# A fixed table of operations in place of a list scheduler, and ReLU and square in one tile

## Chip, core, metric

One core of a Trainium2 chip. The metric is the device time of the kernel in microseconds (us), as the median of several runs.

## What is computed

Linear attention with cosine weights, followed by a feed-forward layer with a squared ReLU. Everything arrives in float32; the kernel multiplies in bfloat16.

```python
q, k, v: (8, 8, 576, 64)           # batch, heads, positions, head size
w_in: (512, 2048)   w_out: (2048, 512)

theta = pi / 2 * pos / S
phi(x) = concat([relu(x) * cos(theta), relu(x) * sin(theta)], -1)
kv  = einsum('bhsf,bhsd->bhfd', phi(k), v)
z   = sum over s of phi(k)
num = einsum('bhsf,bhfd->bhsd', phi(q), kv)
den = einsum('bhsf,bhf->bhs', phi(q), z) + 1e-6
x = (num / den), as 4608 tokens of 512
out = (relu(x @ w_in) ** 2) @ w_out
```

## The kernel before

**Work and names.** The kernel handles the eight batches one after another, each 512 tokens ("main"); the last 64 positions of all batches ("tails") are gathered as a ninth block, number 8. Every piece of work is an operation of a planner (`plan.op`) with a name, the engines that may run it and a cost on each, the operations that it follows, and the buffers that it holds. The engines are TensorE (PE), VectorE (DVE), ScalarE (ACT), GpSimd (POOL) and SyncE (SP). Names for batch b:

- `ldk`, `ldq`, `ldv`, `ldkt`, `ldqt`: loads of k, q, v and of the tails of k and q, issued by SP (by POOL for the first batches). k and q share one buffer (`kq`), of which there is one, so a batch's load waits for the last feature of the batch before.
- `vs`: v spread into the operand of the attention product; `cosb.j`, `sinb.j` (`fe` in the profile, lines 525 and 527): the features of k and q for a quarter of the positions, on ACT or DVE; `.t` is the tail.
- `qTd`, `xTd`: transposes by DMA on SP's queue; `qT`, `xT` with `qTc`, `xTc`: transposes by TensorE and the copy behind them (the first two batches).
- `kv`, `kvz`: the sum of phi(k) v, and its copy; `num`, `div`: the numerator on TensorE and the division on DVE (three instructions).
- `Hb.s.th`: a plain product x @ w_in for tokens half t and half h of the hidden units, block s (batches 0, 1 and half of 2), with its ReLU `r` and its square `q`.
- `Gb.s`: the same for four such products by a seven-product scheme (Strassen's form, as Winograd rearranged it): `P1` to `P7` on TensorE, `seed`, `u2`, `s5` copies out of PSUM between them, and four results `c11`, `c12`, `c21`, `c22`, each with a ReLU `r` and a square `q`. `xs` are the sums of blocks of x, `w1s`, `w2t` those of the weights.
- `Yb`: the second product, by the same scheme: `S1` to `S4` are sums of blocks of the squares, `P1` to `P7` the products, `seed`, `u2`, `s5`, `c..` the copies, `st0`, `st1` the stores. In batch 0 it is plain: `Y0.0` to `Y0.15`. Batch 8's last products, copies and stores are cut in halves.

A product of a G block is four 128x256 matmuls, one of a Y block sixteen. `yb`, `ya`, `hb`, `ha`, `hc`, `hps` in the profile are the PSUM tiles of these products. There are six PSUM banks of the kind that they use (pool `x`) and one more, two banks wide, for `kz` and `num` (pool `n`).

**ReLU and square.** `activate` (line 962) takes a tile `rt` from a pool of four, writes the ReLU of a product's 512 columns into it, and squares it into a part of `gT`, the operand of the second product: `gT` is laid out as token quarter, hidden block, 128 tokens, and the square turns the order:

```python
r = plan.op(f"{name}r", engines, lambda e: emit(e, rt[:, :, :]), after, bufs + [rt])
split = lambda ap: ap.rearrange("p h (t c) -> p t h c", t=2)
g_ready[b, tok, half, s] = plan.op(
    f"{name}q", both(act(2 * W), 0.34),
    lambda e: square(e, g[:, :, 2 * s : 2 * s + 2, :], split(rt[:, :, :])), [r], [rt, g])
```

There are 144 such squares. `gT` has eight blocks; a batch takes four.

**The order.** `Plan.timeline` gives each TensorE step a due time along a planned sequence, `Plan.dues` passes due times back to what it needs, and `Plan.run` (line 208) plays a list scheduler: at every moment each free engine takes, of the operations that are ready and whose buffers have room, the one with the earliest due time plus a hand-set shift (`SHIFT`); an operation that ACT and DVE can both do goes to the one that ends it first, or where `PINS` puts it. Each engine then runs its operations in that order, each waiting for what it needs, so that whatever stands behind a waiting instruction on the same engine waits too. The orders that come out, where they are spoken of below:

```
TensorE  H1.3.01 H1.1.00 num2.2 H1.3.11 H1.2.11 num2.3 Y1.P1 num2.0 Y1.P2 num1.4 Y1.P6 Y1.P5
TensorE  num3.2 G2.3.P1 G2.3.P5 Y1.P3 num3.3 G2.2.P7 G2.2.P3 xT1.4 Y1.P4 num2.4
         G2.3.P2 G2.3.P6 G2.2.P4 G2.3.P7 Y2.P1
TensorE  Y2.P7 G3.1.P4 G3.2.P2 num3.4 G3.2.P6 G3.3.P1 Y2.P3
DVE      G3.1.c22r sin5.0 G3.1.c22q G3.1.c21r Y2.c22
SP       qTd4.0 qTd4.1 xTd2.2 Y1.st1 ldqt6.0 ldv5.0 ldkt6.1 ldk5 ldq5 ldkt6.0
```

Of the kernel before, what the change touches and what calls it, by code (L numbers as in the profile page):

```python
# [17 lines left out]
FP = 512  # L18

LAG = {"PE": 0.21, "ACT": 0.15, "DVE": 0.14, "POOL": 0.15, "SP": 0.1}  # L20
SAME = 0.12
CARE = 1.0
ROOM = 2500
SHIFT = {
    "H0.0.00.0": 23.3, "H0.0.10.0": 65.1, "H0.2.10.0": 67.9, "H0.3.01.0": 100.8, "sin1.0": 16.7,
    "sin1.2": 46.1, "num1.0": 22.3, "qT1.3": -67.9, "num1.3": 71.9, "num1.4": 80.8,
    "Y0.13": 67.3, "ldv2.2": -46.8, "ldkt2.0": -47.2, "num2.0": 98.2, "xTd2.1": 24.1,
    "H1.0.10.0": 14.7, "H1.1.00.0": 64.8, "H1.2.00.0": -21.4, "H1.2.11.0": 97.2,
    "H1.3.01.0": 43.2, "H1.3.11.0": 93.2, "vs3.1": 33, "cos3.2": 20.4, "sin3.t": 42.9,
    "div3.4": 15.5, "xs2.2": 40.2, "H2.0.10.0": 15.6, "H2.0.01.0": -24.5, "H2.1.00.0": -45.7,  # L30
    "H2.1.01.0": 9, "H2.1.11.0": 5.4, "G2.2.u2": 38.7, "G2.2.P3": 32.8, "G2.2.c12q": 8.6,
    "G2.2.P7": 25.3, "G2.2.c22r": 2.7, "G2.3.seed": -10.2, "Y1.S4": 32.8, "Y1.P7": 7,
    "Y1.P3": 13.8, "Y1.c12": -77.9, "Y1.P4": 24, "vs4.1": 37.5, "sin4.0": -4.1, "cos4.1": 5.5,
    "sin4.2": -74.7, "sin4.3": -4.2, "num4.2": -19, "div4.4": 37.7, "xTd4.2": 147.6,
    "G3.0.P1": -10.2, "G3.0.P5": -64.2, "G3.0.P2": -4, "G3.0.P6": -9.8, "G3.0.P3": -41.8,
    "G3.0.P4": -12.3, "G3.1.P1": -64.3, "G3.1.seed": -8.5, "G3.1.P6": -36.7, "G3.1.P3": -20.1,
    "G3.2.P1": -23.4, "G3.2.P6": 12.1, "G3.2.c22r": 9.4, "G3.3.c11q": 22.3, "G3.3.c12r": 6.4,
    "G3.3.c22q": 19.6, "G3.3.c21q": 3, "Y2.P6": 3.7, "Y2.P5": -7.6, "Y2.P3": 15.5,
    "Y2.st0": 52.3, "Y2.st1": 80.4, "ldk5": 45.3, "ldq5": 53.1, "ldv5.0": 29.5, "vs5.1": 8.5,
    "cos5.0": 3.1, "div5.0": 17.6, "num5.1": 18.6, "div5.1": 47.3, "num5.4": 16, "G4.0.P5": 23.7,  # L40
    "G4.0.P3": -47.4, "G4.2.P1": 20.1, "G4.2.P2": 11.4, "G4.2.s5": 39.5, "G4.2.c12r": 1.7,
    "G4.2.P4": -80, "G4.3.P1": -53.6, "G4.3.P4": -11, "Y3.P6": 12.5, "Y3.P3": 16.9,
    "Y3.st0": 43.4, "Y3.st1": 134.8, "ldv6.0": 71.2, "ldv6.2": 38.3, "ldkt6.0": 32.6,
    "ldqt6.0": -5.7, "ldqt6.1": 37.9, "cos6.0": 38.4, "cos6.2": 46.4, "sin6.2": 28.5,
    "sin6.3": 32.6, "qTd6.1": 47.7, "num6.4": -23.5, "xs5.1": 11.7, "xs5.2": 3.2, "xs5.4": -19.2,
    "G5.0.P3": -36.7, "G5.1.P5": -13, "G5.1.c12r": 29.6, "G5.1.c22r": -21.5, "G5.2.P1": 3.5,
    "G5.2.P5": 8.1, "G5.2.P2": 1.8, "Y4.S4": -92.6, "Y4.S3": -85.2, "Y4.P1": -1.2, "Y4.P7": 35.4,
    "Y4.P5": -3.4, "ldk7": 116.4, "ldkt7.0": 40.2, "ldkt7.1": 34.3, "G6.0.P3": 49.7,
    "G6.1.P5": 41.4, "G6.2.P2": 47.4, "G6.2.P6": 48.2, "G6.2.P3": 68.3, "G6.2.c21r": 40.2,
    "G6.3.P5": 44.3, "G6.3.P2": 60.8, "Y5.P4": 42.1, "G7.0.P7": 38.8, "G7.1.P5": 46.8,  # L50
    "G7.2.P6": -13.6, "G7.3.P6": -4.6, "G7.3.c21r": 7, "Y6.P6": 65.2, "Y6.P7": 79.3,
    "Y6.P4": 26.7, "G8.0.P2": 34.1, "G8.0.s5": 3.7, "G8.1.P7": 33.7, "Y7.P6": 130.6,
    "Y7.P7": 241.7, "Y7.P4": 300.4,
}
EARLY = 20
STRETCH = 1.08
EARLY_TAIL = 15
REPORT = []
PLAIN = ((1, 0), (1, 1), (2, 0))
PINS = {  # L60
    "ACT": (
        "qTc0.3 H0.3.01q sin1.0 cos1.1 sin1.1 cos1.3 sin1.3 vs2.1 H1.0.11r H1.1.00r H1.3.01q "
        "sin3.0 cos3.3 cos3.t H2.0.01q H2.1.00r G2.3.u2 G2.3.s5 sin4.1 cos4.2 cos4.3 G3.0.s5 "
        "G3.1.c11q G3.2.c11r G3.3.c12q G3.3.c21r cos5.t sin5.t G4.0.c12q G4.1.c21q G4.2.u2 "
        "G4.2.c12q G4.3.c12q G4.3.c22q Y3.c21 vs6.1 sin6.1 cos6.3 G5.2.u2 G7.0.c12q Y7.s5"
    ),
    "DVE": (
        "vs3.1 cos3.2 G3.1.c21r G3.2.u2 cos5.1 cos5.2 cos5.3 G4.1.c11q G4.1.c22q G4.1.c21r "
        "G4.2.s5 G4.3.c21q cos6.0 cos6.2 G5.1.c22q G5.1.c21r G7.2.c22q G7.3.c21r Y6.u2 "
        "G8.0.c21r"  # L70
    ),
}
PIN = {n: e for e, names in PINS.items() for n in names.split()}
BIAS = 0
EITHER = ("ACT", "DVE")


class Buf:
# [3 lines left out]
    def __init__(self, pool, shape, dtype, name, kind=None):  # L82
        self.pool, self.shape, self.dtype, self.name, self.kind = pool, shape, dtype, name, kind
        self.users, self.left, self.slot, self.tile = [], 0, None, None
# [39 lines left out]
class Op:  # L124
    def __init__(self, name, engines, emit, after, bufs, due, done, slack, fixed):
        self.name, self.engines, self.emit, self.bufs = name, engines, emit, bufs
        self.after = [a for a in after if a is not None]
        self.due, self.done, self.slack, self.fixed = due, done, slack, fixed
        self.next, self.start, self.end, self.engine, self.late = [], None, None, None, None
        for a in self.after:  # L130
            a.next.append(self)
        for b in bufs:
            b.users.append(self)


class Plan:
# [3 lines left out]
    def __init__(self):  # L140
        self.ops, self.pools, self.fifo = [], {}, {}

    def pool(self, name, n, order=None):
        self.pools[name] = n
        if order is not None:
            self.fifo[name] = order

    def op(self, name, engines, emit, after=(), bufs=(), due=None, done=None, slack=0.0):
        o = Op(name, engines, emit, after, list(bufs), due, done, slack, None)
        self.ops.append(o)  # L150
        return o

    def given(self, name, at, bufs=()):

        o = Op(name, {}, None, (), list(bufs), 0.0, None, 0.0, at)
        self.ops.append(o)
        return o

    def timeline(self, chains, at):

        for row in chains:
            todo = [list(c) for c in row]
            size = max(len(c) for c in todo)
            taken = [0] * len(todo)
            for n in range(1, size + 1):
                for i, c in enumerate(todo):
                    while taken[i] < len(c) * n // size:
                        o, drains = c[taken[i]]
                        taken[i] += 1
                        o.due = at  # L170
                        at += o.engines["PE"] * STRETCH
                        for d, slack in drains:
                            d.due = at + slack

    def dues(self):

        after = {o: list(o.after) for o in self.ops}
        for p in self.fifo:
            made = self.order(p) if self.fifo[p] == 1 else []
            for old, new in zip(made, made[self.pools[p] :]):  # L180
                users = set(new.users)
                for o in new.users:
                    if not users.intersection(o.after):
                        after[o] += old.users
        later = {o: [] for o in self.ops}
        for o in self.ops:
            for a in after[o]:
                later[a].append(o)
        count = {o: len(later[o]) for o in self.ops}
        todo = [o for o in self.ops if not count[o]]  # L190
        while todo:
            o = todo.pop()
            if o.fixed is not None:
                continue
            took = min(o.engines.values())
            if o.done is not None:
                took += o.done[0] + CARE
            late = min((n.due - 0.15 for n in later[o]), default=1e6) - took
            if o.late is not None:
                late = min(late, max(a.due for a in o.after) + o.late)  # L200
            o.due = late if o.due is None else min(late, o.due)
            o.due -= o.slack
            for a in after[o]:
                count[a] -= 1
                if not count[a]:
                    todo.append(a)

    def run(self, free, dma=0.0):


        taken = {(b.pool, b.slot) for o in self.ops for b in o.bufs if b.slot is not None}
        slots = {
            p: [(0.0, i) for i in range(n) if (p, i) not in taken] for p, n in self.pools.items()
        }
# [4 lines left out]
        for o in self.ops:  # L219
            o.key = o.due + SHIFT.get(o.name, 0.0)  # L220
# [1426 lines left out]
```

## Time and profile before

| what | value |
|---|---|
| time, median of 3 runs | 277.29 us (277.2 to 278.34) |
| span of the profiled execution | 275.1 us |
| first matmul, of the warm-up | 1.2 us |
| last matmul starts | 270.8 us |
| idle time of ACT ahead of features, for q (the longest) | 6.7 us (3.3) |
| idle time of DVE ahead of features, for k and for q | 5.2 and 3.2 us |
| moved by DMA | 53.00 MB |

The span runs from the first to the last instruction of one execution; the time of a run has some two microseconds more around it. A row of the timeline or of the groups names the engine, the source line, the operation and the tiles it writes and reads; a bracket gives the idle time of the engine ahead of it and what ended that. Matmuls overlap, so their recorded time is longer than the distance between their starts. Many operations have one helper's line (538 is every matmul, 509 every copy), so they are told apart by their tiles and their order.

### The profile page before, as it was taken

What the parts mean: (1) busy time and instruction counts of PE and PEld (TensorE: products, weight loads), DVE (VectorE), ACT (ScalarE), POOL (GpSimd) and SP (SyncE); (2) the same over time, 40 slices, a digit from 0 to 9 for tenths busy, and PEclk for the clock granted to TensorE, in tenths of its full rate; (3) what the DMA queues carried; (4) which work ended last, traced back from release to release, by engine and by line L of the source; (5) the groups of instructions that cost most, each with busy time, mean ns of one, the idle gap of its engine ahead of it and who ended that gap; (6) DMA issues with size and microseconds to landing.
All of it is one profiled execution on the core that took longest, in us unless ns stands there. A gap on an engine that the chain in (4) does not pass through costs nothing.

```text
span 275.1 us, 6864 instructions
## 1 busy us (share of the span) xinstructions
PE 266.3 (97%) x2792; PEld 225.1 (82%) x2792; DVE 229.6 (83%) x449; ACT 190.3 (69%) x322; POOL 28.7 (10%) x47
## 2 busy tenths in 40 slices
PE   8999999999999999989999999999999999999994
PEld 2579746699798888968998999888988888888883
DVE  2778677998999899979999899989779889977931
ACT  5587791798698589779898877888358744665400
POOL 8834364100000000000000000000000000000000
PEclk9999999999999999999999999999999999999999
DMA  7999999999999997999986999483321001100125
GB/s 225 293 206 259 311 284 273 355 285 271 303 232 345 268 186 219 349 163 191 327 255 172 246 235 305 99 219 119 79 100 63 4 12 67 79 0 2 76 57 174
DMA packets 79198, 53.00 MB, mean 193 GB/s; under 512 B 52256, under 2 KB 74784, under 8 KB 79168
## 3 DMA queue, kind: packets, MB, share of 16 engines
q1 hardware_dynamic: 71488, 38.28, 54.5%
q0 software_dynamic: 7040, 13.76, 19.2%
q10 hardware_dynamic: 640, 0.52, 0.7%
q8 instruction: 22, 0.36, 0.5%
q14 instruction: 8, 0.07, 0.1%
HBM read 36.70 MB, written 9.44 MB: 168 GB/s over the span
## 4 chain that ended last, share of the span: by engine, by line
PE 69%; DMA 18%; DVE 4%; POOL 4%; ACT 3%; issue 1%; SPq 1%; DVEq 0%; POOLq 0%; ACTq 0%
PE ya L538 15%; PE yb L538 13%; PE hb L538 10%; DMA kq<-in_q_dram 7%; PE hc L538 7%; PE ha L538 7%; PE hps L538 6%; DMA w1sb<-in_moe_w_in_dram 5%; PE yh L538 4%; DMA kqt<-in_k_dram 3%; PE kz L538 2%; PE num L538 2%; DMA qpTt<-fet 2%; DVE gs L535 1%; PE yc L538 1%; ACT fe L525 1%
## 5 line engine op out<-in xcount | busy, mean ns | idle before, releaser
L538 PEld LDWEIGHTS <-w1sb 128*128 128x128 bf16 x736 | 70.1, 98 | 10.5 <-issue 2.4
L538 PEld LDWEIGHTS <-gs 128*128 128x128 bf16 x512 | 49.7, 98 | 6.1 <-DVE gs L535 0.4
L538 PEld LDWEIGHTS <-gT 128*128 128x128 bf16 x448 | 43.3, 98 | 10.7 <-issue 0.5
L519 ACT ACTIVATE gT<-rt 128x512 bf16<-128x512 bf16 x65 | 40.4, 630 | 8.5 <-DVE rt L532 7.0
L525 ACT ACTIVATE fe<-kq,cols 128x1024 bf16<-128x1024 f32 (+1 forms) x34 | 34.2, 1043 | 9.2 <-DMA kq<-in_q_dram 6.7
L538 PE MATMUL hps<-xT,w1sb 128*128 128x256 bf16 x320 | 37.5, 273 | 0.0
L521 DVE TENSOR_TENSOR gT<-rt 128x512 bf16<-128x512 bf16 x79 | 31.7, 420 | 3.5 <-ACT rt L513 3.1
L527 DVE TENSOR_SCALAR fe<-kq,cols 128x1024 bf16<-128x1024 f32 (+1 forms) x38 | 25.9, 718 | 8.4 <-DMA kq<-in_k_dram 5.2
L538 PEld LDWEIGHTS <-w1s 128*128 128x128 bf16 x312 | 29.8, 98 | 3.6
L538 PE MATMUL ya<-w2sb,gT 128*128 128x256 bf16 x256 | 30.7, 273 | 0.4 <-ACT yb L509 0.4
L538 PE MATMUL hb<-xs,w1sb 128*128 128x256 bf16 x208 | 30.4, 273 | 0.4 <-ACT u L509 0.2
L538 PE MATMUL ha<-xT,w1sb 128*128 128x256 bf16 x176 | 25.9, 273 | 1.3 <-DVE rt L515 1.2
L670 DVE TENSOR_TENSOR xp<-num,den 128x512 bf16<-128x512 f32 (+1 forms) x33 | 22.2, 675 | 1.1
L513 ACT ACTIVATE rt<-hps 128x512 bf16<-128x512 f32 x34 | 19.7, 596 | 4.5 <-PE hps L538 4.3
L535 DVE TENSOR_TENSOR gs<-gT 128x2048 bf16<-128x2048 bf16 x16 | 19.5, 1220 | 0.3 <-ACT gT L519 0.2
L532 DVE CUSTOM_DVE_ANT_0 rt<-hc,u 128x512 bf16<-128x512 f32 x26 | 17.6, 684 | 2.6 <-PE hc L538 2.6
L532 DVE CUSTOM_DVE_ANT_0 rt<-hb,s 128x512 bf16<-128x512 f32 x26 | 17.8, 686 | 1.4 <-PE hb L538 1.1
L513 ACT ACTIVATE rt<-ha 128x512 bf16<-128x512 f32 x23 | 13.7, 595 | 6.3 <-PE ha L538 6.3
L509 ACT COPY u<-hb 128x512 f32<-128x512 f32 x22 | 12.8, 583 | 4.9 <-PE hb L538 4.7
L509 ACT COPY s<-hc 128x512 f32<-128x512 f32 x20 | 11.8, 588 | 6.4 <-PE hc L538 6.3
L509 ACT COPY hb<-ha 128x512 f32<-128x512 f32 x26 | 15.3, 590 | 0.6 <-PE ha L538 0.3
L538 PE MATMUL hc<-xs,w1s 128*128 128x256 bf16 x104 | 15.6, 273 | 0.0
(112 smaller groups left out, 411.1 us busy)
## 6 DMA issues: line engine op xcount, KB each, us to landing
out_dram<-y SPq DMA_DIRECT2D x16, 512.0 KB, 4.3
vs<-in_v_dram SPq DMA_DIRECT2D x10, 512.0 KB, 4.9
kq<-in_k_dram SPq DMA_DIRECT2D x5, 1024.0 KB, 6.8
kq<-in_q_dram SPq DMA_DIRECT2D x5, 1024.0 KB, 9.0
w1sb<-in_moe_w_in_dram POOLq DMA_DIRECT2D x4, 512.0 KB, 11.5
w2sb<-in_moe_w_out_dram POOLq DMA_DIRECT2D x4, 512.0 KB, 11.2
kq<-in_q_dram POOLq DMA_DIRECT2D x2, 1024.0 KB, 10.9
kq<-in_k_dram POOLq DMA_DIRECT2D x2, 1024.0 KB, 11.4
```

Source lines behind the costliest of these rows:

```text
L509: (nc.scalar.copy if e == "ACT" else nc.vector.tensor_copy)(out=out, in_=in_)
L513: nc.scalar.activation(out=out, in_=in_, func=ACTF.Relu)
L519: nc.scalar.activation(out=out, in_=in_, func=ACTF.Square)
L521: nc.vector.tensor_tensor(out=out, in0=in_, in1=in_, op=ALU.mult)
L525: nc.scalar.activation(out=out, in_=in_, func=ACTF.Relu, scale=col)
L527: nc.vector.tensor_scalar(out=out, in0=in_, scalar1=0.0, scalar2=col, op0=ALU.max, op1=ALU.mult)
L532: nc.vector._custom_dve(dve_ops.TENSOR_ADD_SAT, out=out, in0=in0, in1=in1, s0=BIG, s1=0.0)
L535: nc.vector.tensor_tensor(out=out, in0=in0, in1=in1, op=op)
L538: nc.tensor.matmul(out=out, lhsT=lhsT, rhs=rhs, start=start, stop=stop, skip_group_check=True)
L670: nc.vector.tensor_tensor(out=x, in0=n4[:, :, :, 0:D].rearrange("p b (k l) d -> p b k l d", l=2), in1=r.rearrange("p b (k l) -> p b k l", l=2)
```

## The change

**The order is a table.** `SHIFT`, `PINS`, the due times, `timeline`, `dues`, `order` and the list scheduler go. A string `ORDER` lists all 1066 operations; a star puts one on ACT where ACT and DVE could both do it. `Plan.run` walks through it and only chooses the slot of each new buffer:

```diff
+    def run(self, table, free, dma=0.0):
+        ops = {o.name: o for o in self.ops}
+        order = []
+        for word in table.split():
+            o = ops.pop(word.rstrip("*"))
+            o.engine = "ACT" if word[-1] == "*" else min(o.engines, key=lambda e: e == "ACT")
+            order.append(o)
...
+        for o in order:
+            e = o.engine
+            t = max([free[e]] + [a.end + lag(a, e) for a in o.after])
+            for b in sorted((b for b in o.bufs if b.slot is None), key=lambda b: b.index):
+                t, b.slot = slot(b, t)
```

The estimated costs that the planner uses are set anew (`act(n)` from 0.14 to 0.08 us plus 0.00082 per element, `dve(n)` from 0.10 to 0.07 plus 0.00104, and the like); they now serve the choice of slots alone. Which products are plain and which are by the scheme stays as it was, and so does all that is issued ahead of the plan (`begin`, `loads_of_1`).

**ReLU and square in one tile.** `gT` is laid out as hidden block, token quarter, 128 tokens; the ReLU writes straight into it, and one square works in place on two neighbouring blocks. The pool `rt` goes.

```diff
-                gT[b, tok, half] = buf("g", [P, 2, HB2, P], BF16, "gT")
+                gT[b, tok, half] = buf("g", [P, HB2, 2, P], BF16, "gT")
...
-        rt = buf("rt", [P, 2, W], BF16, "rt")
         g = gT[b, tok, half]
-        r = plan.op(f"{name}r", engines, lambda e: emit(e, rt[:, :, :]), after, bufs + [rt])
...
+        many = SQUARES.get(b, 2)
+        r = plan.op(
+            f"{name}r", engines, lambda e: emit(e, g[:, 2 * s : 2 * s + 2, :, :]), after, bufs + [g]
+        )
+        group = squares.setdefault((b, tok, half, s // many), [])
+        group.append(r)
+        if len(group) < many:
+            return r
+        s0 = s // many * many
+        part = slice(2 * s0, 2 * (s0 + many))
...
+            lambda e: square(e, g[:, part, :, :], g[:, part, :, :]),
+            group,
+            [g],
```

`SQUARES` is empty, so `many` is 2 everywhere: 72 squares of 1024 elements a partition. The sums `gs` of the second product and its matmuls take the new layout; the matmuls are the same in number and size. The tile of zeros for the warm-up moves from the place of `rt` to that of `gs`.

**The order in the table**, at the places quoted above and at some others (the table isn't sorted by time; what counts is the order on each engine):

```
TensorE  H1.3.11 num2.2 H1.1.00 H1.2.11 num2.3 H1.3.01 Y1.P1 num2.0 Y1.P2 num1.4 Y1.P6 Y1.P5
TensorE  num3.2 Y1.P3 G2.2.P3 xT1.4 G2.2.P7 num3.3 G2.3.P1 Y1.P4 num2.4
         G2.3.P2 G2.3.P6 G2.3.P5 G2.2.P4 G2.3.P7 Y2.P1
TensorE  Y2.P7 G3.1.P4 num3.4 G3.2.P6 G3.2.P2 G3.3.P1 Y2.P3
TensorE  G4.3.P1 G4.2.P3 G4.3.P5 G4.3.P6      Y3.P7 G4.2.P6 G4.2.P2 num4.4 Y3.P4
TensorE  G7.3.P6 G7.2.P4 G8.0.P1 G7.3.P7
DVE      G3.1.c22r div4.3 sin5.1 G3.1.c21r cos5.2
ACT      sin4.0 G2.3.c11r G2.3.u2 G2.3.s5 Y1.c21 G2.2.c21r cos4.3 cos4.t G3.0.seed
ACT      G6.1.s5 G6.1.c11q G6.2.seed G6.1.c12q G6.3.seed    G6.3.c11q G7.0.seed    G7.3.c22q G8.0.seed
SP       qTd4.0 Y1.st0 xTd2.2 qTd4.1 ldv5.0 ldk5 ldq5 ldkt6.0 Y1.st1 xTd4.0
```

## Prediction

> **What bounds the kernel now.** I read the page's busy times first, then the table by stretches, then the TensorE timeline with its waits, then the queues behind the waits that are left.
>
> ```profile
> span 275.1 us, 6864 instructions
> PE 266.3 (97%) x2792; PEld 225.1 (82%) x2792; DVE 229.6 (83%) x449; ACT 190.3 (69%) x322; POOL 28.7 (10%) x47
> ```
>
> ```profile
> core 0: us, PE busy (x) PEld busy (x) DVE busy (x) ACT busy (x) POOL busy (x), PEclk, DMA share, GB/s
> ...
> 36.00:70.00 34.00, 33.62 (x381) 25.61 (x380) 28.89 (x59) 24.98 (x40) 7.54 (x11) 1.00 1.11 296
> 70.00:95.00 25.00, 23.98 (x281) 21.20 (x279) 23.02 (x45) 18.05 (x29) 0.00 (x0) 1.00 1.11 279
> 95.00:121.00 26.00, 24.28 (x279) 20.92 (x277) 23.11 (x48) 21.05 (x37) 0.00 (x0) 1.00 1.09 252
> 121.00:160.00 39.00, 39.00 (x449) 34.94 (x448) 37.22 (x76) 34.01 (x57) 0.00 (x0) 1.00 0.89 233
> ...
> 200.00:240.00 40.00, 40.00 (x374) 35.83 (x372) 35.88 (x67) 24.33 (x45) 0.00 (x0) 1.00 0.14 54
> ```
>
> TensorE (PE) is the bound. From 121 us to 271 us it has no idle time in any stretch, so no order can gain anything there; it can only lose. The clock is granted in full everywhere. The change issues the same matmuls, so all that can be won is the idle time of TensorE between 16 us (first work after the warm-up) and 121 us. The rows that hold it:
>
> ```profile
> 71.13 1.91 PE L538 MATMUL ya<-w2sb,gT 128*128 128x256 bf16 x16 [0.41 <-ACT yb L509]
> ...
> 73.54 1.92 PE L538 MATMUL yb<-w2t,gs 128*128 128x256 bf16 x16 [0.26 <-DVE gs L535]
> ...
> 93.80 0.27 PE L693 MATMUL tx<-ident,xpt 128*128 128x128 bf16 x2 [0.34 <-DVE y L535]
> ...
> 97.36 0.60 PE L538 MATMUL hb<-xs,w1sb 128*128 128x256 bf16 x4 [0.19 <-DVE rt L532]
> 98.17 0.60 PE L538 MATMUL hb<-xs,w1sb 128*128 128x256 bf16 x4 [0.21 <-ACT u L509]
> ...
> 120.28 0.60 PE L538 MATMUL ha<-xT,w1sb 128*128 128x256 bf16 x4 [1.18 <-DVE rt L515]
> ```
>
> The bracket is shorter than the time lost. A 128x256 matmul is recorded as 273 ns, but four of them start within 0.437 us (a product of four takes 0.44 us in the chain of waits, sixteen take 1.75 us), 0.109 us each, so each record ends 0.16 us after TensorE could have gone on; a 65-column one likewise. I add 0.16 us to each: 0.57, 0.42, 0.50, 0.35, 0.37 and 1.34 us. With 0.54 us at 37.02 (the transpose of batch 1's query tail, idle 0.38 us behind a DVE feature) that is 4.1 us, the most the change can win.
>
> The rule that speaks here is in the Trainium skill, "Perfetto Trace Analysis", Identifying the Most-Contended Engine: matmul busy time flatters TensorE, weight-load busy time does not. By the page PEld is 82%, which looks like 50 us of room; but in the stretch without a wait it is 35.83 of 40 us, so 90% is its ceiling here, 225.1 / 0.896 = 251 us would be the floor, and of the remaining 24 us 20 lie before 16 us and after 271 us. By the rule so read 4 us could be won, as by the gaps.
>
> The largest gap has this behind it (SP's queue, then DVE's):
>
> ```profile
> 107.48 0.60 SPq L578 DMA_DIRECT2D kq<-in_k_dram  x1
> 108.12 0.74 SPq L578 DMA_DIRECT2D kq<-in_q_dram  x1
> ...
> 118.53 0.75 DVE L527 TENSOR_SCALAR fe<-kq,cols 128x1024 bf16<-128x1024 f32 x1 [1.60 <-DMA kq<-in_q_dram]
> ...
> 119.54 0.69 DVE L515 TENSOR_SCALAR rt<-hb 128x512 bf16<-128x512 f32 x1
> ```
>
> Batch 5's q lands 10.3 us after its issue. DVE stands at a feature of that batch; the ReLU G3.1.c21r queued behind it frees the bank that G3.3.P1 needs.
>
> **The change part by part.**
>
> *The squares.* Rows:
>
> ```profile
> L519 ACT ACTIVATE gT<-rt 128x512 bf16<-128x512 bf16 x65 | 40.4, 630 | 8.5 <-DVE rt L532 7.0 <-DVE rt L515 0.7
> L521 DVE TENSOR_TENSOR gT<-rt 128x512 bf16<-128x512 bf16 x79 | 31.7, 420 | 3.5 <-ACT rt L513 3.1
> L535 DVE TENSOR_TENSOR gs<-gT 128x2048 bf16<-128x2048 bf16 x16 | 19.5, 1220 | 0.3 <-ACT gT L519 0.2
> L509 ACT COPY qpT<-tq 128x1024 bf16<-128x1024 bf16 x1 | 1.0, 1012 | 0.4 <-ACT xT L509 0.4
> L535 DVE TENSOR_TENSOR w1sb<-w1sb 128x2048 bf16<-128x2048 bf16 x1 | 1.2, 1218 | 0.0
> ```
>
> 144 squares of 512 elements become 72 of 1024; counted by the stars in the table, 41 are on ACT and 31 on DVE. No row has a 1024-element square. On DVE a line through 512 (0.420) and 2048 (1.220) gives 0.42 + 512 x 0.000521 = 0.69 us; bounds: 0.42 from below, two old ones, 0.84, from above. Working in place costs nothing by the last row (1.218 beside 1.220 us). On ACT the nearest row, 1024 elements at 1.01 us, and the 128x1024 features at 1.14 us bound it; I take 1.04 us. DVE: 79 x 0.42 = 33.2 becomes 31 x 0.69 = 21.3 us. ACT: 65 x 0.63 = 41.0 becomes 41 x 1.04 = 42.6 us. The rest of the table moves three ReLUs, three features and one spread of v from ACT to DVE and one copy the other way, so DVE loses about 8 us of work in all, ACT about 1. TensorE waits for neither engine after 121 us, so this work is under cover and is worth 0 to TensorE directly; if the cover is gone (a square stands ahead of an eviction) see the second rival. The ReLU itself writes as many contiguous elements as before: 0. Its new target means that it waits for a block of the squares instead of one of four rt tiles; that block was last read by the products of two batches earlier, long done: 0.
>
> *The order on TensorE.* Both orders have the same 363 steps, and they are near neighbours. I count, for each step of a seven-product block that needs an eviction of an earlier step, the TensorE work that stands between. At 71.13 such a round trip shows: the product's stream ends at about 70.31 and the next starts at 71.13, 0.82 us. Of 168 such places 21 have less than 1.5 us of cover before and 19 after. Gap by gap:
> - 37.02: the same work stands ahead on TensorE (Y0.0 to Y0.3) and on DVE (two features, then the tails). It stays.
> - 71.13: Y1.P1, num2.0, Y1.P2 again. It stays.
> - 73.54: Y1.P6 waits for Y1.S2, that for Y1.S1, that for the squares of token half 1. The last ReLU block of that half, H1.2.11, now has H1.3.01 (0.87 us) between it and Y1.P1. 0.42 us won.
> - 93.80: the transpose of x's tail waits for a PSUM bank. Before, G2.3.P1 and G2.3.P5 already held one each; in the table both come after it, so a bank is open. 0.50 us won.
> - 97.36 and 98.17: G2.2.P4 and G2.3.P7 wait for evictions. G2.3.P5 (0.44 us) now stands between. Of 0.72 us I count 0.60 won.
> - 120.28: SP's queue. Before, the store Y1.st1 and the tail loads ldqt6.0 and ldkt6.1 stood between the transposes of batch 4 and ldk5 (104.26 to 107.48 us). In the table ldv5.0, ldk5, ldq5 follow qTd4.1 directly and those three come later. What remains ahead is the last feature of batch 4 (cos4.3, now behind G2.2.c21r on ACT: the product G2.2.P4 starts at 97.36, plus 0.6, a ReLU of 0.6 and a feature of 1.14, about 99.7 us), qTd4.1 (half of the 3.82 us of two, 1.9 us) and the load of v (0.57 us): ldk5 at about 102.5 us, 5 us earlier. With the same 10.3 us the batch lands at about 113.5 us, before DVE comes to it (116.93 us, where its wait of 1.60 us began). 1.34 us won; bounds 0 and 1.34. The stores moved back are waited for by no engine soon: the tile y is next written a batch later.
>
> Won: 0.42 + 0.50 + 0.60 + 1.34 = 2.9 us.
>
> *New waits.* Three places after 121 us have less cover than any there before: G4.3.P6 (4.26 to 0.87 us), G7.3.P7 (1.31 to 0.87) and Y3.P4 (1.64 to 1.20), against a round trip of 0.82 us with nothing queued ahead. Bounds 0 and one square each, 3 x 0.63; I take 0.4 us together, since two of three still cover the bare trip by 0.05 us.
>
> *Unchanged:* the loads and warm-up before 16 us, and the 4.1 us after the last matmul (a copy, a store, its landing).
>
> Sum: 275.1 - 2.9 + 0.4 = 272.6 us of span. The median of the runs is 277.29 us, 2.2 us over the span, so **274.8 us**, 0.9% faster.
>
> **Rivals.**
>
> *No change.* New waits take what the old ones give back. For it: the stretch of 150 us without a wait is not forgiving, and 19 places have under 1.5 us of cover. Against it: there were 21 before, and they cost nothing. If the landing of batch 5 also gains only half: 277.3 - 2.2 + 2.0 = 277.1 us.
>
> *Slower: long squares on ACT ahead of evictions.* ACT runs strictly in the table's order, and its squares grow from 0.63 to 1.04 us, 0.41 us more. In the table 13 evictions that a product waits for (such as G6.3.seed behind G6.1.c12q, G7.0.seed behind G6.3.c11q, G8.0.seed behind G7.3.c22q) stand directly behind one. If each is late by that much and its cover is spent: 13 x 0.41 = 5.3 us, and 277.3 - 2.9 + 5.3 = 279.7 us. It decides when such a square begins less than its length, less the spare cover (1.31 - 0.82 = 0.49 us), before the eviction's input is ready. Against it: ACT is idle 39 to 58% of the time after 200 us (24.33 busy of 40 us, then 12.97 of 31), so most squares will be over by then.
> Its rule is in the Trainium skill, "Perfetto Trace Analysis", Optimizing Scalar/DVE Operations: grouping helps an engine that is saturated, breaking up helps where an engine is not saturated but makes others wait. DVE at 23.02 of 25 us is of the first kind; ACT at 18.05, with the wait at 71.13, is of the second, so by the rule this half of the change goes the wrong way.
>
> *The table doesn't do what it says:* it was laid out for landings that come later here, and the features of batches 4 to 7 stop DVE and ACT as those of batch 5 do. Three further batches at 1.34 us: 277.3 - 1.5 + 4.0 = 279.8 us. Against it: the waits for batches 6 and 7 are absent before.
>
> **How the numbers follow.** Under 0.5% (1.4 us) a measurement of this kernel can't tell from no change. Forecast (faster, 272.9 to 275.9): 0.58. No change (275.9 to 278.7): 0.22. Slower through ACT: 0.14; through landings: 0.06. All 4.1 us won and nothing lost gives 273.2 us, and 0.4 us of the smaller gaps of that stretch gives 272.8, the low end. The high end takes in the smaller half of the slower cases, 279.0 us. The forecast's own range is 272.9 to 275.9.
>
> **What would show it.** Right: no wait of TensorE near 94 and 97 us, q of batch 5 issued before 105 us and no DVE wait for it, one wait of 0.4 us at Y1.P2 left, TensorE without idle time from about 118 to 268 us; DVE busy about 222 us, squares at 0.69 and 1.04 us. Wrong: new rows of TensorE idle after 121 us released by ACT copies (second rival), or by DVE or ACT features behind a DMA (third).

## The result and the profile after

| kernel | median, us (lowest to highest, runs) | ratio to the kernel before, 95% interval |
|---|---|---|
| before, beside it | 277.31 (277.2 to 278.34, 6) | 1 |
| changed | 280.25 (278.48 to 282.83, 6) | 1.0084 (1.006 to 1.0108) |

The ratios, here and below, go by the undisturbed runs alone (the 282.83 us is not among them), so a ratio and two medians can differ. By its ratio the changed kernel is slower by 0.84%, 2.3 us, and by the medians 2.9 us, where 2.5 us faster was forecast. The profiled execution of the changed kernel took 279.37 us, with a span of 276.8 us, 1.7 us over that of before; so its trace explains a little less than the medians differ. First its page: the span, the busy times, and the groups of the squares.

```profile
span 276.8 us, 6802 instructions
...
PE 265.8 (96%) x2788; PEld 224.9 (81%) x2792; DVE 224.2 (81%) x407; ACT 190.9 (69%) x292; POOL 28.7 (10%) x47
...
L422 ACT ACTIVATE gT<-gT 128x1024 bf16<-128x1024 bf16 x41 | 43.0, 1059 | 2.0 <-DVE gT L435 0.9
...
L424 DVE TENSOR_TENSOR gT<-gT 128x1024 bf16<-128x1024 bf16 x31 | 20.8, 685 | 1.1 <-ACT gT L416 0.9
```

The work came out as it was costed: 41 squares of 1.059 us on ACT and 31 of 0.685 us on DVE, and DVE has 5.4 us less to do. The table by stretches (busy us of PE, PEld, DVE, ACT, POOL; granted clock; DMA) shows that none of it reached the end. The last row is of the kernel before:

```profile
95.00:121.00 26.00, 23.05 (x265) 20.34 (x265) 21.15 (x41) 19.81 (x33) 0.00 (x0) 1.00 0.98 259
121.00:160.00 39.00, 39.00 (x449) 34.90 (x448) 36.83 (x70) 34.30 (x51) 0.00 (x0) 1.00 0.94 234
160.00:200.00 40.00, 38.81 (x434) 34.35 (x433) 35.55 (x69) 26.81 (x41) 0.00 (x0) 1.00 0.79 161
200.00:240.00 40.00, 40.00 (x374) 35.58 (x372) 31.93 (x51) 27.31 (x44) 0.00 (x0) 1.00 0.17 56
...
160.00:200.00 40.00, 40.00 (x452) 35.48 (x450) 35.68 (x72) 29.73 (x50) 0.00 (x0) 1.00 0.70 164
```

TensorE is still the bound, but it is idle 2.95 us between 95 and 121 us (1.72 before) and 1.19 us between 160 and 200 us, where it had no idle time at all. The granted clock is 1.00 in every row. Its timeline names the two places:

```profile
100.45 0.19 PE L441 MATMUL kz<-vext,fe 128*128 128x65 bf16 x1
103.47 1.09 PE L441 MATMUL kz<-vext,fe 128*128 128x65 bf16 x31 [2.82 <-DVE vext L412]
...
174.13 0.32 PE L441 MATMUL num<-kvz,qpTt 128*64 128x65 bf16 x8 [1.00 <-DVE xp L573]
```

Measured from start to start, less what the matmul in front takes to stream, the gaps are 2.98 us (kv4, the product of batch 4's keys and values) and 1.17 us (a numerator of batch 6). With the same measure, gap by gap, from 30 us on:

| place in the kernel before | before, us | changed, us |
|---|---|---|
| 37.02, transpose of batch 1's query tail | 0.54 | none |
| 71.13, Y1.P1, copy, Y1.P2 | 0.58 | 0.58 |
| 73.54, Y1.P6 | 0.42 | none |
| 93.80, transpose of x's tail | 0.51 | none; 0.40 at the next product |
| 97.36 and 98.17, G2.2.P4 and G2.3.P7 | 0.36 and 0.37 | 0.29 |
| 120.28, G3.3.P1 | 1.34 | none |
| kv4, at 100.45 | none | 2.98 |
| numerator of batch 6, and the product behind it, at 172.86 | none | 1.17 and 0.35 |

Closed: 0.54 + 0.42 + (0.51 - 0.40) + (0.73 - 0.29) + 1.34 = 2.85 us. New: 4.50 us, and 0.51 us more at 21.71, where an early load of w1 lands. The last matmul starts 1.64 us later (272.40 against 270.76), 0.5 us less than these gaps add up to; that rest lies in steps too small to read one by one.

What stands behind kv4 are two queues. The first is SP's, the second DVE's:

```profile
93.57 0.53 SPq L491 DMA_DIRECT2D vs<-in_v_dram  x1
94.20 3.16 SPq L494 DMA_DIRECT2D vst<-in_v_dram  x2
97.41 0.61 SPq L484 DMA_DIRECT2D kqt<-in_k_dram  x1
98.11 1.28 SPq L618 DMA_TRANSPOSE xT<-xp  x1
99.49 1.32 SPq L609 DMA_TRANSPOSE qpTt<-fet  x1
```

```profile
102.33 0.49 DVE L430 TENSOR_SCALAR fet<-kqt,cols 128x512 bf16<-128x512 f32 x1 [3.16 <-DMA qpTt<-fet]
102.73 0.69 DVE L412 CAST vext<-vs 128x1024 bf16<-128x1024 f32 x1
```

The same places in the kernel before, on SP, DVE and ACT:

```profile
96.28 1.22 SPq L706 DMA_TRANSPOSE qpTt<-fet  x1
...
100.57 0.68 DVE L509 CAST vext<-vs 128x1024 bf16<-128x1024 f32 x1
...
100.73 1.33 ACT L525 ACTIVATE fet<-kqt,cols 128x512 bf16<-128x512 f32 x2 [1.15 <-DMA qpTt<-fet]
```

The tail features of a batch have one tile, `fet`. Batch 4's (cos4.t and sin4.t) may be written only when qTd3.2 has read batch 3's. In the kernel before both stood on ACT, which waited 1.15 us, and no product with it. The table moves sin4.t to DVE, ahead of vs4.1, the spread of v that kv4 needs. DVE stands still for 3.16 us, v with it, TensorE with both. (ACT stands at cos4.t for 2.88 us at the same time.) The transpose is also later: it issues at 99.49 us, where the kernel before issued it at 96.28. Two loads, ldv5.2 and ldkt5.1, now stand between the transposes of batch 3 ahead of it; whether they are what makes it late is tested below. Behind the second gap SP's and DVE's queues look like this:

```profile
155.53 6.80 SPq L609 DMA_TRANSPOSE qpT<-fe  x1
162.38 0.57 SPq L481 DMA_DIRECT2D kq<-in_q_dram  x1
163.00 0.57 SPq L481 DMA_DIRECT2D kq<-in_k_dram  x1
```

```profile
172.29 0.75 DVE L430 TENSOR_SCALAR fe<-kq,cols 128x1024 bf16<-128x1024 f32 x1 [2.45 <-DMA kq<-in_k_dram]
...
173.39 0.69 DVE L573 TENSOR_TENSOR xp<-num,den 128x512 bf16<-128x512 f32 x1
```

A feature of batch 7 (cos7.1) waits 2.45 us for the load of k, and the division of batch 6, which the numerator's product needs, is queued behind it. That load isn't later than before. In the kernel before it goes out at 163.34 us and lands 9.3 us later, as here, but the division stands ahead of the feature on DVE:

```profile
163.34 0.42 SPq L578 DMA_DIRECT2D kq<-in_k_dram  x1
...
170.35 0.69 DVE L670 TENSOR_TENSOR xp<-num,den 128x512 bf16<-128x512 f32 x1
...
172.82 1.41 DVE L527 TENSOR_SCALAR fe<-kq,cols 128x1024 bf16<-128x1024 f32 x2
```

So at the second gap the order on DVE is what is new.

### The profile page after: what moved, and what is told of

The parts are those of the page before. It is cut to its first block, busy times and chain, and to the rows that moved or that the text cites. A ratio compares the mean times of both kernels' runs of the same rounds, so it can differ in the third digit from the quotient of the medians.

```text
span 276.8 us, 6802 instructions
## 1 busy us (share of the span) xinstructions
PE 265.8 (96%) x2788; PEld 224.9 (81%) x2792; DVE 224.2 (81%) x407; ACT 190.9 (69%) x292; POOL 28.7 (10%) x47
## 4 chain that ended last, share of the span: by engine, by line
PE 81%; DMA 9%; POOL 3%; DVE 3%; issue 1%; ACT 1%; SPq 0%; POOLq 0%; DVEq 0%
PE ya L441 17%; PE yb L441 14%; PE hps L441 12%; PE hb L441 11%; PE hc L441 7%; PE ha L441 7%; PE yh L441 5%; DMA w1sb<-in_moe_w_in_dram 5%; DMA kq<-in_k_dram 3%; PE kz L441 3%; PE num L441 3%; PE yc L441 1%; DMA qpTt<-fet 1%; PE tq L591 1%; DVE fe L430 1%
## 5 line engine op out<-in xcount | busy, mean ns | idle before, releaser
L422 ACT ACTIVATE gT<-gT 128x1024 bf16<-128x1024 bf16 x41 | 43.0, 1059 | 2.0 <-DVE gT L435 0.9
L428 ACT ACTIVATE fe<-kq,cols 128x1024 bf16<-128x1024 f32 (+1 forms) x36 | 36.7, 1052 | 3.9 <-DMA kq<-in_k_dram 1.8
L430 DVE TENSOR_SCALAR fe<-kq,cols 128x1024 bf16<-128x1024 f32 (+1 forms) x36 | 24.0, 704 | 7.7 <-DMA kq<-in_k_dram 6.4
L424 DVE TENSOR_TENSOR gT<-gT 128x1024 bf16<-128x1024 bf16 x31 | 20.8, 685 | 1.1 <-ACT gT L416 0.9
L435 DVE CUSTOM_DVE_ANT_0 gT<-hb,s 128x512 bf16<-128x512 f32 x26 | 17.7, 684 | 4.8 <-PE hb L441 4.0
L435 DVE CUSTOM_DVE_ANT_0 gT<-hc,u 128x512 bf16<-128x512 f32 x26 | 17.8, 685 | 2.7 <-PE hc L441 1.7
L416 ACT ACTIVATE gT<-hps 128x512 bf16<-128x512 f32 x29 | 16.4, 600 | 4.8 <-PE hps L441 4.6
L416 ACT ACTIVATE gT<-hb 128x512 bf16<-128x512 f32 x20 | 11.7, 595 | 10.0 <-PE hb L441 9.9
L416 ACT ACTIVATE gT<-ha 128x512 bf16<-128x512 f32 x22 | 13.1, 597 | 5.5 <-PE ha L441 5.5
L441 PE MATMUL hb<-xs,w1s 128*128 128x256 bf16 x104 | 15.6, 273 | 0.0
```

The lines of the kernel that those rows point to most:

```text
L416: nc.scalar.activation(out=out, in_=in_, func=ACTF.Relu)
L422: nc.scalar.activation(out=out, in_=in_, func=ACTF.Square)
L424: nc.vector.tensor_tensor(out=out, in0=in_, in1=in_, op=ALU.mult)
L428: nc.scalar.activation(out=out, in_=in_, func=ACTF.Relu, scale=col)
L430: nc.vector.tensor_scalar(out=out, in0=in_, scalar1=0.0, scalar2=col, op0=ALU.max, op1=ALU.mult)
L435: nc.vector._custom_dve(dve_ops.TENSOR_ADD_SAT, out=out, in0=in0, in1=in1, s0=BIG, s1=0.0)
```

## The experiments

Two theories. **Queues**: the new order puts steps that wait for a transpose or a load ahead of steps that TensorE needs, and the squares are free. **Squares**: the long squares hold up what stands behind them. All times are medians, each beside runs of the kernel before on the same chip (277.5 to 278.1 us). The kernels ran on several chips, so a difference between two of them is safer by their ratios, where 0.1% is 0.28 us.

### Order and squares apart

`old_order_pairs`: the planner's order of the kernel before written out as a table, each engine's sequence kept, but with the merged squares in place, each where the square of its second block stood, which is the later of the two in 63 of 72 (six had to go behind a ReLU).

```diff
-ORDER = """ (the new table)
+ORDER = """ (the sequence of the kernel before, 72 squares of 1024)
```

> The table mechanism with the order and the engines that the list scheduler had given, and the new squares (in place, two blocks at once, where the second of the two stood). If the loss comes from the order (two waits: kv4 behind a late transpose, 3.0 us, and batch 7's load, 1.5 us): as the kernel before, 276.5 to 278.0 us, and the old waits of TensorE at 71, 73, 94, 97 and 120 us are back. If the long squares cause it: slower than before by 2 to 3 us, about 280 us, with new waits behind squares after 121 us.

282.22 us, ratio 1.0146 (1.0092 to 1.02). Squares won this one, and by more than it asked: in the old order the change of the squares costs as much as the whole change does, or more (1.46% against 0.84%, intervals that overlap). TensorE's timeline has three new gaps:

```profile
67.87 0.40 PE L438 MATMUL num<-kvz,qpT 128*128 128x65 bf16 x8 [0.55 <-DVE xp L570]
...
106.45 0.60 PE L438 MATMUL ha<-xT,w1sb 128*128 128x256 bf16 x4 [1.02 <-ACT gT L413]
...
136.27 0.60 PE L438 MATMUL hc<-xT,w1s 128*128 128x256 bf16 x4 [0.90 <-ACT s L409]
```

`new_order_singles`: the new table, each merged square split into two of 512 at the same point.

```diff
-SQUARES = {}
+SQUARES = {b: 1 for b in range(9)}
```

> The new order, but each square of 1024 elements is done as two of 512, in place, one after the other at the same point of the table. If the order is the cause: as the changed kernel or up to 1 us slower, 279.5 to 281.5 us, the waits near 100 and 173 us still there. If long squares were the cause: near 277 us, and those two waits gone or halved.

280.59 us, 1.0098 (1.0068 to 1.0128), with 1.40 us lost at kv4 and 1.19 us at batch 6's numerator. In the new order the length of the squares makes no measurable difference; the loss is the order's, which here includes the engine that each operation runs on.

`old_order_singles`: the old order as a table, all 144 squares at their old places, in place.

> The order of the kernel before on every engine, written as a table, with all 144 squares of 512 elements at their old places, in place in the tile of the ReLU. It differs from old_order_pairs only in that no squares are merged. If merging is what cost there (the three gaps at 67, 105 and 135 us, 0.72, 1.19 and 1.06 us): these gaps are under 0.4 us each and the time is that of the kernel before, 276.5 to 278.5 us. If it is what both share (the slots chosen by the table's walk, the square in place, the missing rt tiles): the gaps stay and the time is 281 to 283 us.

277.99 us, 0.9992 (0.9965 to 1.0018). The table, the slots it chooses, the square in place and the missing `rt` cost nothing that can be measured. Merging costs 282.22 - 277.99 = 4.2 us in the order that was laid out for short squares (4.3 us by the ratios).

### The two waits of the new order

`tail_transpose_first` and `load7_first` change SP's queue alone:

```diff
-ldv4.1 ldv5.2 ldkt5.1 xTd3.1 qTd3.2 qTd4.0 Y1.st0 xTd2.2 qTd4.1
+ldv4.1 xTd3.1 qTd3.2 qTd4.0 Y1.st0 xTd2.2 qTd4.1 ldv5.2 ldkt5.1
```

> The changed kernel with two loads of batch 5's tails (ldv5.2, ldkt5.1) moved on SP's queue from ahead of xTd3.1 and qTd3.2 to behind qTd4.1. If kv4 waits because qTd3.2 is late: qTd3.2 is issued by 96 us in place of 99.5, the wait of 2.82 us of TensorE near 100 us falls under 0.8 us, and the time falls by 2 to 3 us against the changed kernel, to about 277.7 us. If v's own load (ldv4.1) is what is late: the wait stays over 2 us, time about 280 us.

279.10 us, 1.004 (1.0001 to 1.008): a miss. The transpose issues at 97.97 us, not by 96, and the gap at kv4 is 1.70 us, not under 0.8. In the five profiles of the new order in which neither SP's queue ahead of the transpose nor `fet` was changed (the changed kernel's two, `new_order_singles`, `load7_first`, `cos7_later`) the transpose issues between 98.28 and 99.49 us and the gap is 1.40 to 2.98 us. So it isn't shown that the two loads made the transpose late. And the loads that were put back are now ahead of batch 5's, whose q comes late again: a gap of 1.0 us at 119.8. The interval overlaps with that of the changed kernel, so no gain is shown either.

```diff
-qTd6.1 ldq7 ldk7
+ldq7 qTd6.1 ldk7
```

> The changed kernel with batch 7's load of q moved ahead of the transpose qTd6.1 on SP's queue, as it stood before the change. If the DVE feature cos7.1 standing for k of batch 7 causes the waits near 173 and 176 us: q is issued near 156 us in place of 162.4, DVE's wait of 2.45 us falls under 0.5 us, TensorE's two waits (1.5 us with their overlap) go, time about 278.8 us; the wait near 100 us stays. If those waits come from something else on DVE: no change, about 280 us.

280.87 us, 1.0123 (1.0069 to 1.0178): the gap at 172 is gone, and one of 1.13 us stands at 168.4, where a numerator waits for qTd6.1. Only q was moved. k, which the feature waits for, went out at 166.10 us, later than the 163.00 of the changed kernel, and DVE still waits 1.30 us for it. An earlier k wasn't run.

So the next three leave SP alone. `two_fet` takes away what sin4.t waits for, `cos7_later` what stands ahead of the division, `two_fet_cos7` does both:

```diff
-    pool("fet", 1, 2048)
+    pool("fet", 2, 2048)
```

```diff
-cos7.1 ... div6.3 ... G5.1.c12r G5.1.c12q ... Y4.c12
+div6.3 ... G5.1.c12r G5.1.c12q ... Y4.c12 cos7.1
```

> The changed kernel with two tiles fet in place of one, order untouched: batch 4's tail features no longer wait until the transpose qTd3.2 has read batch 3's. If the wait ahead of kv4 (2.98 us at 100.45 us) comes from the one tile fet, by way of sin4.t on DVE: DVE's wait of 3.16 us at sin4.t is gone, the gap is under 0.9 us and the time is 2 us below the changed kernel, 278.0 to 278.8 us. If v's load or SP's queue itself is what kv4 waits for: the gap stays over 2 us and the time at 280 us.

277.82 us, 1.0024 (0.999 to 1.0057): 1.7 us below the changed kernel by the ratios (2.4 by the medians). The interval just parts from that of the changed kernel (from 1.006) and just meets that of its second set of runs, below (from 1.0055). In DVE's timeline tail feature and spread run without a wait, and kv4 with them, although the transpose issues at 98.22 us, still behind the two loads. TensorE waits 0.63 us for a sum of x right behind kv4, and 1.68 us at 107.6, at a numerator that needs qTd4.1 (3.17 us on SP's queue there, 1.58 in the changed kernel's profile):

```profile
98.59 0.48 DVE L427 TENSOR_SCALAR fet<-kqt,cols 128x512 bf16<-128x512 f32 x1
98.99 0.69 DVE L409 CAST vext<-vs 128x1024 bf16<-128x1024 f32 x1
```

```profile
109.38 0.42 PE L438 MATMUL num<-kvz,qpT 128*128 128x65 bf16 x8 [1.52 <-DMA qpT<-fe]
```

> The changed kernel with one step moved on DVE: the feature cos7.1, which waits for k of batch 7, goes from ahead of div6.3 to behind Y4.c12. If the gap of 1.17 us at 172.86 us comes from that feature standing ahead of the division: num6.4's product no longer waits, no gap over 0.4 us between 160 and 180 us, and the time is 0.9 to 1.2 us below the changed kernel, 279.0 to 279.4 us. If the landing only stops the next thing (as load7_first did): a new gap of 0.5 to 1.2 us after 172 us, 280 us.

279.07 us, 1.0035 (1.0011 to 1.0059): 1.4 us below the changed kernel by the ratios, with an interval that again parts from the first and meets the second. The numerator waits no longer, but a product two steps on is 0.80 us late.

> Both together, the changed kernel with two tiles fet and cos7.1 behind Y4.c12. If the two waits are what the new order costs and are independent: 3 us below the changed kernel, 276.8 to 277.8 us, that is level with the kernel before, because the gaps that the new order closed (2.9 us by the prediction) are then offset by smaller new ones and not by these two. If TensorE loses the time elsewhere whatever is done here: over 279 us.

277.94 us, 1.0000 (0.9975 to 1.0026): with both waits dealt with, the changed kernel is level with the kernel before, not below. Its profile has the two gaps no more, but 1.09 us at 95.1, 0.67 us at 108.9. Its interval is clear of both sets of runs of the changed kernel. Of the 4.2 us of the two gaps 2.3 us came back in time.

> The changed kernel itself, instruction for instruction, beside the others on one chip. If its two waits (kv4 at 100 us, the division of batch 6 at 172 us) are what it always does: 279.5 to 281 us, both gaps there, each within 1 us of the first profile (2.98 and 1.17 us). If they were chance of one execution: one of them under 0.4 us and another in its place.

279.59 us, 1.0089 (1.0055 to 1.0123). Both waits are there again, 1.99 and 0.88 us, and 0.95 us at 95.1 (0.40 in the first profile): the places are the same, the sizes differ between executions.

`five_moves` adds three moves to `two_fet_cos7`: ldv5.2 and ldkt5.1 behind ldq5, cos4.2 behind the copy G2.3.seed, G3.1.c21r ahead of sin5.1.

> The changed kernel with two tiles fet, cos7.1 behind Y4.c12, ldv5.2 and ldkt5.1 behind ldq5 on SP, cos4.2 behind the copy G2.3.seed on ACT and G3.1.c21r ahead of sin5.1 on DVE: every wait over 0.5 us that the profiles of the new order showed between 90 and 180 us is met by one move. If the new order's remaining loss is these queue places: no gap over 0.6 us between 90 and 180 us, and 275 to 276.5 us, below both kernels. If the landings, which come at other times in each execution, stop TensorE at some other step: gaps of 0.5 us or more remain, and 277 to 278.5 us.

278.09 us, 1.0013 (0.9992 to 1.0034): a miss. Gaps of 0.67 us at 94.1 and 1.32 us at 96.4 remain, the latter at a product that waits for a copy on ACT, which stands behind the feature that I moved.

### The largest term of the prediction, alone

`old_load5_first`: `old_order_singles` with one move on SP.

```diff
-qTd4.1 xTd2.2 Y1.st1 ldqt6.0 ldv5.0 ldkt6.1 ldk5 ldq5
+qTd4.1 ldv5.0 ldk5 ldq5 xTd2.2 Y1.st1 ldqt6.0 ldkt6.1
```

> old_order_singles with one step moved on SP: ldv5.0, ldk5 and ldq5 directly behind qTd4.1, ahead of xTd2.2, Y1.st1, ldqt6.0 and ldkt6.1, as in the changed kernel. It tests the largest term of the prediction (1.34 us won at 120 us) by itself. If that term holds: the gap ahead of G3.3.P1 (1.34 and 1.74 us at 119 us in the kernel before and in old_order_singles) is under 0.3 us and the time is 1 to 1.5 us below old_order_singles, 276.4 to 277.2 us. If the gain is taken back at once by later landings: the gap is gone, another of 0.5 us or more follows before 130 us, and the time stays at 277.7 to 278.2 us.

276.55 us, 0.9961 (0.9932 to 0.9991). It is below both kernels. SP's queue of `old_order_singles` and then of this one:

```profile
107.81 0.60 SPq L484 DMA_DIRECT2D kq<-in_k_dram  x1
108.45 0.76 SPq L484 DMA_DIRECT2D kq<-in_q_dram  x1
```

```profile
103.43 0.58 SPq L484 DMA_DIRECT2D kq<-in_k_dram  x1
104.05 0.58 SPq L484 DMA_DIRECT2D kq<-in_q_dram  x1
```

and the feature on DVE that waits for q, in the same two:

```profile
119.23 0.75 DVE L433 TENSOR_SCALAR fe<-kq,cols 128x1024 bf16<-128x1024 f32 x1 [2.01 <-DMA kq<-in_q_dram]
```

```profile
116.52 0.75 DVE L433 TENSOR_SCALAR fe<-kq,cols 128x1024 bf16<-128x1024 f32 x1
```

The load goes out 4.4 us earlier, the wait of 2.01 us is gone, and TensorE's gap of 1.74 us at 119 with it.

> old_load5_first once more, the same instructions: base of the three runs beside it. If its gain is real: a ratio of 0.994 to 0.998 to the kernel before, about 276.6 us. If it was chance: 0.998 to 1.002.

276.22 us, 0.9933 (0.99 to 0.9965): the gain over the kernel before is real. `load5_two_fet`, with a second `fet` tile:

> old_load5_first with two tiles fet. In the old order ScalarE waited 1.15 us at a feature for the transpose qTd3.2, and no product waited for it. If that wait was covered there: level with the base within 0.4 us. If it is part of what holds up the evictions at 97 us: those gaps (0.35 and 0.37 us) fall under 0.2 us and the time is 0.3 to 0.6 us below the base.

276.60 us, 0.9959 (0.9929 to 0.9989): level. In the old order the wait for the one tile was under cover.

### Which merged squares cost

`old_pairs_moved`: `old_order_pairs` with five squares moved behind what they stood ahead of.

```diff
-H1.3.00q H1.3.10q H1.1.10q div2.1 ... G2.3.c22q G3.0.seed ... G3.3.c12q G4.0.u2 G4.0.s5
+div2.1 H1.3.00q H1.3.10q H1.1.10q ... G3.0.seed G2.3.c22q ... G4.0.u2 G4.0.s5 G3.3.c12q
```

> old_order_pairs with five of its 72 long squares moved behind what stood behind them: three on DVE behind the division div2.1, G2.3.c22q on ACT behind the copy G3.0.seed, G3.3.c12q on ACT behind the copies G4.0.u2 and G4.0.s5. If a long square costs by the place it has in its engine's queue: the gaps at 67, 105 and 135 us (0.72, 1.19, 1.06 us) are under 0.4 us each and the time falls from 282.2 by 2 to 3 us, to 279 to 280 us. If long squares cost through their work or their later finish for the sums: the gaps come back elsewhere and the time stays at 281.5 us or more.

282.44 us, 1.0176 (1.015 to 1.0202): a miss for the theory of five places. (Its profiled run took 286.76 us, so I read no gap from it.) The cost doesn't sit in those five alone.

So the 72 pairs were sorted by where their two squares stood, and each kind was merged by itself on top of `old_load5_first`, at the place of the second square (where an odd block's comes first, at the later one):

```diff
-        many = SQUARES.get(b, 2)
+        many = 2 if f"{name[:3]}{s // 2 * 2 + 1}{name[4:]}" in MERGE else 1
```

> old_load5_first with 20 of the 72 pairs of squares merged, those whose two squares both stand on VectorE, at the place of the second; VectorE is spared 20 x 0.15 us. If only long squares on ScalarE cost (the second rival): 0 to 0.4 us below the base, 276.2 to 276.7 us. If the later finish of the first square costs wherever it is: 0.5 us or more above the base, 277.2 us or more, with waits of TensorE for gT of VectorE's squares.

> old_load5_first with the 13 pairs merged whose two squares both stand on ScalarE, at the place of the second. If long squares on ScalarE cost by standing ahead of evictions: 0.7 us or more above the base, 277.3 to 278.5 us, with new gaps of TensorE released by ScalarE copies or ReLUs. If what costs in old_order_pairs are the 39 pairs that change engine or move far: level with the base, 276.3 to 276.9 us.

> old_load5_first with the 21 pairs merged whose first square stood on VectorE and whose second on ScalarE: all of both now on ScalarE (21 x (1.05 - 0.63) = 8.8 us more work there). If the second rival is right, long squares on ScalarE ahead of evictions: 1.5 to 3 us above the base, 277.8 to 279.2 us, with TensorE waiting for ScalarE's copies and ReLUs. If each merge costs alike (0.03 us, as in the two runs before): 276.9 to 277.4 us.

> old_load5_first with the 18 pairs merged whose first square stood on ScalarE and whose second on VectorE: all now on VectorE, the busier of the two (18 x (0.69 - 0.42) = 4.9 us more work there). If the second rival is right and the cost is ScalarE's: level with the base within 0.6 us, 276.3 to 277.0 us. If work moved to the busier engine costs: 1 to 2 us above the base, 277.4 to 278.6 us, with TensorE waiting for VectorE's results.

| pairs merged | us | ratio, 95% interval | over the base (276.4, mean of its two medians) |
|---|---|---|---|
| 20, both on VectorE | 276.83 | 0.9955 (0.9931 to 0.9978) | 0.4 |
| 13, both on ScalarE | 276.96 | 0.9963 (0.994 to 0.9987) | 0.6 |
| 21, one moved to ScalarE | 278.35 | 1.0009 (0.9983 to 1.0036) | 2.0 |
| 18, one moved to VectorE | 277.02 | 0.997 (0.9936 to 1.0004) | 0.6 |

By the medians they add up to 3.6 us, against 4.2 for all pairs in the old order without the earlier load; by the ratios (0.2, 0.4, 1.7 and 0.6 us over the mean of the base's two) to about 3.0 against 4.3. More than half comes with the pairs of which one square moved to ScalarE, where the work itself grows as well as the length. The three smaller rows overlap with the base's interval and with each other; only the third stands apart (from `load5_again` by its interval, from `old_load5_first` all but). One stretch of ACT shows how, in `load5_again` and then in `load5_merge_to_act`:

```profile
128.02 0.59 ACT L419 ACTIVATE gT<-hb 128x512 bf16<-128x512 f32 x1
128.50 1.15 ACT L425 ACTIVATE gT<-gT 128x512 bf16<-128x512 bf16 x2
129.55 0.59 ACT L415 COPY yb<-ya 128x512 f32<-128x512 f32 x1
130.06 0.63 ACT L425 ACTIVATE gT<-gT 128x512 bf16<-128x512 bf16 x1
...
131.05 0.60 ACT L415 COPY s<-hc 128x512 f32<-128x512 f32 x1
```

```profile
129.04 0.59 ACT L422 ACTIVATE gT<-hb 128x512 bf16<-128x512 f32 x1
129.52 2.00 ACT L428 ACTIVATE gT<-gT 128x1024 bf16<-128x1024 bf16 x2
131.42 0.59 ACT L418 COPY yb<-ya 128x512 f32<-128x512 f32 x1
131.93 1.06 ACT L428 ACTIVATE gT<-gT 128x1024 bf16<-128x1024 bf16 x1
...
133.35 0.60 ACT L418 COPY s<-hc 128x512 f32<-128x512 f32 x1
```

```profile
134.00 0.60 PE L447 MATMUL hc<-xT,w1s 128*128 128x256 bf16 x4 [0.90 <-ACT s L418]
```

From the ReLU to the copy of `hc` there are 3.03 us with short squares and 4.31 us with long ones. The copy empties the bank that the product of the last line fills: TensorE's gap there is 1.05 us, the largest in that profile.

## Why the prediction was wrong

The step that failed is **New waits**, put at 0.4 us; it measured 4.5 us in the trace, and those 4.1 us are nearly all of the difference between the span forecast, 272.6 us, and the 276.8 us of the profile. The median lies another 0.9 us above the profiled run. I counted the TensorE work between a product and the copy of its result, looked for thin places after 121 us only, and did nothing else. kv4, at 100 us, isn't such a place: what feeds it is v's spread on DVE, and ahead of that a feature, and ahead of that a transpose on SP. The table had moved sin4.t to DVE, which could be read in it, and I didn't follow it. I had counted the moves between ACT and DVE net, as eight operations; squares aside, the table puts 52 on DVE that stood on ACT and 46 the other way. `two_fet` shows that the one tile is a link of this chain: with a second the gap is gone and 1.7 us come back. That sin4.t's place on DVE is the other link is read from the traces; no run put it back. The second wait is of the same kind, cos7.1 ahead of the division; `cos7_later` shows that place.

**Gaps closed**, put at 2.9 us, measured 2.85 us. But the agreement is partly luck:

- 73.54: right, closed. 71.13: right, it stays, 0.58 us. 37.02: put at staying, and gone in this execution.
- 93.80 and 97: 1.10 us were put in, 0.55 came; the idle time moved to the product after (0.40 us).
- 120.28: closed, but not as I reckoned. I put ldk5 at 102.5 us; it went out at 107.48, the same time as before. My sum let qTd4.1 go as soon as its feature was there, but qTd3.2, qTd4.0, Y1.st0 and xTd2.2 stand ahead of it in the queue, from 99.49 us on, and it issued at 104.82. q went out at 107.91 and landed 9.7 us later, at 117.6; DVE came to it only at 118.48, after it had stood 3.16 us ahead of kv4. So it was luck that this gap closed. Where the load really is early, in the old order, the term holds: 1.74 us in the trace, and by the ratios of its two sets of runs to that of `old_order_singles` 0.9 and 1.6 us of the whole (the interval of the first set overlaps with that of `old_order_singles`, the second just meets it).

**The squares**: durations right (0.685 and 1.059 us for 0.69 and 1.04), DVE's total 224.2 us for "about 222". Worth 0 to TensorE: right in the new order (`new_order_singles` level with the changed kernel), wrong in the old order, where they cost 4.2 us. I argued from the cover that TensorE has after 121 us; the gap of 1.06 us at 135 us lies where I had said the cover was whole.

**The floor by the weight loads**, which seemed to confirm that 4 us could be won, doesn't come out. It counts all 20 us before 16 us and after 271 us as lost, but PEld is busy 7.24 us before 16 us in the trace of the kernel before; at the same 0.896 about 12 us are lost there, and 12 of the 24 us are left, not 4. Nor is 0.896 a ceiling that holds everywhere: from 36 to 70 us PEld is busy 25.61 of 34 us while TensorE is idle for 0.38 us. The 4.1 us rest on the gaps alone.

**The rivals.** *No change* is what comes out once the two waits are dealt with (1.0000). *Slower, long squares on ACT*: its price of 279.7 us was near the result, its cause isn't there: the splits gain nothing in the new order. In the old order its mechanism shows, in the stretch of ACT above. *Slower, features stopped by landings*: 279.8 us with a chance of 0.06 was the nearest to the truth, in the kind of wait, and named the wrong thing that lands: at kv4 it is a transpose that holds a tile, not a load. At cos7.1 it is a load, as it said, though one that lands no later than before. Its one argument against, that batches 6 and 7 made no waits before, was no argument about another order.

The Trainium skill, "Perfetto Trace Analysis", section Optimizing Scalar/DVE Operations, has it that where ScalarE or VectorE isn't saturated but causes idle time on other engines, breaking up instructions may let work be done sooner. The trace agrees in the old order, where ACT is busy 72% in `load5_merge_to_act` and the squares merged onto it cost 2.0 us; it doesn't in the new order, where ACT is busy 69% and splitting its squares gained nothing.

What stays open: the 0.6 us (1.3 by the ratios) between the four kinds together and all pairs; why moving five squares gained nothing in the old order; what makes qTd3.2 late in the new one; and whether an order exists that keeps all gaps of the new table closed and opens none, which `five_moves` didn't find.

## What to carry to other kernels

When an order is changed, list for each product of the bounding engine all it reads, and follow each input back through every in-order queue to a load or a transpose; count a step as moved when anything ahead of it in any of these queues has moved. A feature that waits for a landing is better placed behind what is ready, as in `cos7_later`, and a tile with one buffer is such a wait as well. Ahead of merging small operations, look for what frees a bank right behind the merged one and how much cover it has: the same merge cost 4.2 us in one order and nothing in another, though there too, by the prediction's count, 13 evictions stand directly behind a long square on ACT.

## What the runs showed of the hardware

A DMA transpose holds SP's queue for very different times: qTd6.1 stood 6.80 us in the changed kernel and 8.24 us in the kernel before, a like transpose at 148.97 us 1.63 us in the changed kernel. What sets the time wasn't tested. The same transpose qTd4.1 took 1.58 us in the changed kernel's profile and 3.17 us in that of `two_fet`, where it issued 0.84 us earlier. The idle time at one place varies from execution to execution (kv4 2.98 and 1.99 us in two profiles of the same instructions, and 1.40 to 2.98 us over the five profiles named at `tail_transpose_first`), so a gap that waits for a landing is good to 1 or 1.5 us in one profile here.
